# Down and output projection on two 64-row groups of TensorE, two token rows alternating, with the attention output stored 640 wide

## The chip, the cores and the metric

The kernel runs on one NeuronCore of a Trainium2 chip. The metric is device time in microseconds for one execution, inputs and outputs in HBM. TensorE does matrix products into PSUM (eight banks of 128 partitions x 512 fp32), VectorE (DVE) and ScalarE (ACT) do elementwise work and empty PSUM, GpSimd (POOL) helps at the start, and SyncE (SP) issues nearly all DMAs.

## The reference

One transformer layer with attention and feed-forward in parallel on a LayerNorm of the same input, in bf16. There are 2048 tokens (S), 576 features (D = 32 heads x 18) and a hidden size of 4608 (F).

```python
def _A_ref(x, wqkv, wo):                  # dilated local attention
    H, Dh, W, dil = 32, 18, 8, 2
    q, k, v = split(x @ wqkv)
    idx = pos[:, None] - (arange(W) * dil)[None, :]      # 8 keys: s, s-2, ..., s-14
    mask = idx >= 0
    ...
    attn = softmax(where(mask, q . k[idx] * Dh ** -0.5, -1e9))
    o = attn . v[idx]
    return o.reshape(B, S, D) @ wo

def _B_ref(x, w_gate, w_up, w_down):
    return (silu(x @ w_gate) * (x @ w_up)) @ w_down

xn = _layernorm(x)
return x + _A_ref(xn, wqkv, wo) + _B_ref(xn, w_gate, w_up, w_down)
```

## The kernel before, in words

Token 16p + r lies on partition p as row r, so a row r is a block of 128 tokens, and a shift by 2 tokens is a shift by two rows. A token tile tt is four rows (512 tokens); there are four tiles.

The kernel has a first stage and then four times two stages.

- **QKV projection** (p_row, L270), row by row. LayerNorm is done two rows ahead on DVE, and the normalized rows are transposed into xnT (feature on partition, token along the free axis). Since 576 = 4.5 x 128, the matmuls use two groups of 64 array rows: the 4.5 feature tiles are nine halves of 64, and the last 64 features stand twice in xnT, on partitions 0-63 and 64-127. ACT writes Q into QO (one row of QO is 576 features), and K and V into a ring for the attention.
- **Gate and up** (g_pair, L519), 9 chunks of four hidden blocks for each token tile. Each hidden block j needs a gate bank and an up bank. In the first sweep the lower 64 rows work on gate and the upper 64 on up; in the second sweep they change over, so that each bank receives all nine halves. Since two row groups must not write one bank at once, a fence stands between the sweeps: a POOL no-op that waits for the last matmul of the first sweep and that the first matmul of the second waits for (fence_after, fence_before). g_evac turns a finished block into hT: ACT makes sg = silu(gate) (L530) and copies up to uc (L531), DVE multiplies (L532). sg and uc have four buffers each.
- **Down and output projection** (L567, L570), after the ninth chunk of a tile. For each of the four rows and each column half h of 288, 36 matmuls of hT with wd and 5 of oT (the attention output, transposed) with wo add up in one bank, all with 128 array rows. DVE adds the residual x (L576) and SP stores the row.

oT takes the place of xnT of the same tokens. It is filled by four DMA transposes on SP (L545) when the gate stage of the tile is over; each reads 640 values from QO, that is the 576 of its row and 64 beyond it, which meet zero rows of wo (L166).

The attention itself is a chain of DVE instructions (chain): products with K (L370), sums over 18 features (L375), softmax with one exponential on ACT (L395), products with V (L402) and their sums (L407), the last of which goes back into QO. It is not written out in one piece: a queue (Filler) holds its parts with guessed costs, and dve.pump(us) emits as many parts as fit the given time, after every g_evac (1.4) and ahead of the residual addition of each row in the down stage (8.5). dve.drain emits what is left of a tile's chain ahead of its transposes. Chain tt + 1 is queued during the gate stage of tile tt, at chunk 1.

Weights for gate and up come in two slots, one chunk ahead; wd (nine parts) and wo (18 parts of 32 rows, one for each feature of a head) come in the gate stage of the first tile.

PSUM is a ring of eight banks: a g_pair takes four, a row of the down stage two.

Of the kernel before, what the change touches and what calls it, by code (L numbers as in the profile page):

```python
# [9 lines left out]
bf16 = mybir.dt.bfloat16  # L10
f32 = mybir.dt.float32
ACT = mybir.ActivationFunctionType
ALU = mybir.AluOpType
# [4 lines left out]
P = 128  # L18
H, DH, W, DIL = 32, 18, 8, 2
D = H * DH  # L20
HALF = D // 2
# [3 lines left out]
KT = 5  # L25
DPAD = KT * P
# [3 lines left out]
R = 16  # L30
RT = 4
NTT = R // RT
TT = RT * P
# [37 lines left out]
def kernel(  # L71
# [11 lines left out]
    nc = tc.nc  # L83
# [3 lines left out]
    NF = F // P  # L87
# [3 lines left out]
    out_v = out.rearrange("b (p r) d -> p (b r) d", r=R)  # L91

    const = ctx.enter_context(tc.tile_pool(name="const", bufs=1))
    big = ctx.enter_context(tc.tile_pool(name="big", bufs=1))
    tmp = ctx.enter_context(tc.tile_pool(name="tmp", bufs=1))
# [7 lines left out]
    warm = const.tile([P, 1], f32, name="warm")  # L103

    xnT = big.tile([P, KT, S], bf16, name="xnT")
    QO_t = big.tile([P, R * D + 64], bf16, name="QO")
    QO = QO_t[:, 0:R * D].rearrange("p (r d) -> p r d", d=D)
    Kr = big.tile([P, NRING, D], bf16, name="Kr")
    Vr = big.tile([P, NRING, D], bf16, name="Vr")
    hT = big.tile([P, NF, TT], bf16, name="hT")  # L110
    wd = big.tile([P, NF, D], bf16, name="wd")
    wo = big.tile([P, KT, D], bf16, name="wo")
# [5 lines left out]
    xr = big.tile([P, RT, D], bf16, name="xr")  # L118
# [16 lines left out]
    oT = xnT  # L135
# [26 lines left out]
    for c in range(1, 4):  # L162
        nc.sync.dma_start(xc_b[c], x_v[:, 4 * c:4 * c + 4, :])
    nc.scalar.activation(warm[:], eps_t[:], ACT.Sqrt)
    nc.gpsimd.memset(QO_t[:, R * D:], 0.0)
    nc.gpsimd.memset(wo[64:128, KT - 1, :], 0.0)  # L166
    for ring in (Kr, Vr):
        nc.gpsimd.dma_start(ring[0:1, 0:HALO, :], wz[0:1, :].unsqueeze(1).to_broadcast([1, HALO, D]))

# [13 lines left out]

    def load_wo(d):
        k, row = divmod(d * H, P)
        nc.sync.dma_start(wo[row:row + H, k, :], A_wo.rearrange("(h d) j -> d h j", d=DH)[d])

    def load_wd(ch):
        nc.sync.dma_start(wd[:, ch * FC:(ch + 1) * FC, :],
# [2 lines left out]
    def new_ps(name):  # L192
        return ps.tile([P, 512], f32, name=name, tag="ps")
# [91 lines left out]
    def fence_after(mm):  # L285
        f = nc.gpsimd.engine_nop()
        tc.add_manual_dep(f.ins, mm.ins.name, SYNC, reason="first half done")
        return f

    def fence_before(mm, f):  # L290
        tc.add_manual_dep(mm.ins, f.ins.name, SYNC, reason="banks change row tiles")
# [23 lines left out]
    def p_evac(r, t, between=None):  # L315
# [6 lines left out]

        nc.scalar.copy(QO[:, r, 0:G], t[0][:, 0:G])  # L323
        if between is not None:
            between()
        nc.scalar.copy(ks[:, j, HALF:D], t[2][:, 0:HALF])
        v_copy(0, 8, t[2][:, HALF:G])
        nc.scalar.copy(QO[:, r, G:D], t[1][:, 0:D - G])
        nc.scalar.copy(ks[:, j, 0:HALF], t[1][:, D - G:G])
# [23 lines left out]
    dve = Filler()  # L353
# [7 lines left out]
    def chain(tt):  # L361
        rows = slice(RT * tt, RT * tt + RT)
        prod = PP[:, 0, :].rearrange("p (r c) -> p r c", c=D)
        acc = PP[:, 1, :].rearrange("p (r d h) -> p r d h", d=DH, h=H)
        pv = PP[:, 0, :].rearrange("p (r d h) -> p r d h", d=DH, h=H)
        Lr = L.rearrange("p w r h -> p r h w")

        def mul(w):
            for a, b, s in pieces(tt, w):
                nc.vector.tensor_tensor(prod[:, a:b], QO[:, RT * tt + a:RT * tt + b, :],  # L370
                                        Kr[:, s:s + b - a, :], op=ALU.mult)

        def red(w, h):
            rs = slice(2 * h, 2 * h + 2)
            nc.vector.tensor_reduce(L[:, w, rs], prod[:, rs].rearrange("p r (h d) -> p r h d", d=DH),  # L375
                                    axis=AX.X, op=ALU.add)

        def mask():
            for w in range(1, W):
                n = min(RT, max(0, 2 * w - RT * tt))  # L380
                if n:
                    nc.vector.memset(L[0:1, w, 0:n, :], NEG)

        bc = lambda t: t[:].unsqueeze(1).to_broadcast([P, W, RT, H])
        for w in [0] + list(range(W - 1, 0, -1)):
            dve.add(1.3, lambda w=w: mul(w))
            for h in range(2):
                dve.add(1.2, lambda w=w, h=h: red(w, h))
        dve.add(0.4, mask)
        dve.add(1.2, lambda: nc.vector.tensor_reduce(mx[:], Lr, axis=AX.X, op=ALU.max))  # L390
        dve.add(1.2, lambda: nc.vector.tensor_tensor(L, L, bc(mx), op=ALU.subtract))  # L391
        if tt + 1 < NTT:
            dve.add(0.0, lambda: ring_load(1, tt + 1))
        dve.add(2.0, None)
        dve.add(1.0, lambda: nc.scalar.activation(L, L, ACT.Exp, scale=SCALE))  # L395
        dve.add(1.2, lambda: nc.vector.tensor_reduce(ssum[:], Lr, axis=AX.X, op=ALU.add))  # L396
        dve.add(0.3, lambda: nc.vector.reciprocal(ssum[:], ssum[:]))  # L397
        dve.add(1.2, lambda: nc.vector.tensor_tensor(A[:], L, bc(ssum), op=ALU.mult))  # L398

        def pvm(w, dst):  # L400
            for a, b, s in pieces(tt, w):
                nc.vector.tensor_tensor(dst[:, a:b], Vr[:, s:s + b - a, :].rearrange("p r (d h) -> p r d h", h=H),  # L402
                                        A[:, w, a:b].unsqueeze(2).to_broadcast([P, b - a, DH, H]), op=ALU.mult)

        def pva(w):
            dst = acc if w else QO[:, rows, :].rearrange("p r (d h) -> p r d h", h=H)
            nc.vector.tensor_tensor(dst, acc, pv, op=ALU.add)  # L407

        for w in range(W - 1, -1, -1):
            dve.add(1.4, lambda w=w: pvm(w, acc if w == W - 1 else pv))  # L410
            if w < W - 1:
                dve.add(1.3, lambda w=w: pva(w))
        if tt + 1 < NTT:
            dve.add(0.0, lambda: ring_load(2, tt + 1))

        def done():
            chains[0] += 1
        dve.add(0.0, done)


    def pair_stats(r):
# [37 lines left out]
    for r in range(R):  # L459
        if r == 0:  # L460
            t = p_row0(first)
        else:
            t = p_row(r, (lambda: transp_halves(r + 1)) if r <= 3 else None)
# [61 lines left out]

    def g_evac(ch, j):
        t = ring_ps[j]
        sg = tmp.tile([P, TT], bf16, name="sg", tag="sg", bufs=4)
        uc = tmp.tile([P, TT], bf16, name="uc", tag="uc", bufs=4)
        nc.scalar.activation(sg[:], t[0][:], ACT.Silu)  # L530
        nc.scalar.copy(uc[:], t[1][:])  # L531
        nc.vector.tensor_tensor(hT[:, ch * FC + j, :], sg[:], uc[:], op=ALU.mult)  # L532

    for tt in range(NTT):
        for ch in range(NCH):
            it = tt * NCH + ch
            for p in range(2):
                g_pair(tt, ch, p)
                for j in (2 * p, 2 * p + 1):
                    g_evac(ch, j)  # L540
                    dve.pump(1.4)
            if ch == NCH - 1:
                dve.drain(lambda: chains[0] > tt)
                for r in range(RT * tt, RT * tt + RT):
                    nc.sync.dma_start_transpose(oT[:, :, r * P:(r + 1) * P], QO_t[:, r * D:r * D + KT * P])  # L545
            if it + NSLOT < NTT * NCH:
                load_gu(it + NSLOT)
            if tt == 0:
                if ch == 0:
                    store(1, 3)  # L550
                    store(2, 3)
                if 1 <= ch <= 7:
                    load_wd(ch - 1)
                for _ in range(3 if ch in (1, 2) else 2):
                    if wo_order:
                        load_wo(wo_order.pop(0))
            if ch == 7:
                nc.sync.dma_start(xr[:], x_v[:, RT * tt:RT * tt + RT, :])
            if ch == 1 and tt < NTT - 1:
                chain(tt + 1)  # L560
        for sub in range(RT):
            r = RT * tt + sub
            t = [new_ps("d_ps") for h in range(2)]
            for h in range(2):
                cols = slice(h * HALF, (h + 1) * HALF)
                for f in range(NF):
                    nc.tensor.matmul(t[h][:, 0:HALF], hT[:, f, sub * P:(sub + 1) * P], wd[:, f, cols],  # L567
                                     start=(f == 0), stop=False)
                for k in range(KT):
                    nc.tensor.matmul(t[h][:, 0:HALF], oT[:, k, r * P:(r + 1) * P], wo[:, k, cols],  # L570
                                     start=False, stop=(k == KT - 1))
            dve.pump(8.5)
            ot = tmp.tile([P, D], bf16, name="ot", tag="ot", bufs=3)
            for h in range(2):
                cols = slice(h * HALF, (h + 1) * HALF)
                nc.vector.tensor_tensor(ot[:, cols], t[h][:, 0:HALF], xr[:, sub, cols], op=ALU.add)  # L576
                if r == R - 1:
                    nc.sync.dma_start(out_v[:, r, cols], ot[:, cols])
            if r < R - 1:
                nc.sync.dma_start(out_v[:, r, :], ot[:])  # L580


# [28 lines left out]
```

## Time and profile before

| | |
|---|---|
| three runs | 509.47, 511.37, 513.85 us; median 511.37 |
| profiled execution | 510.26 us, span 508.4 us, granted clock 1.0 |
| TensorE busy | 501.8 us (99%) |
| VectorE, ScalarE busy | 327.3 us (64%), 199.7 us (39%) |
| DMA | 75.01 MB, mean 148 GB/s |
| QKV stage | ends at 62.5 us |
| gate and up, each tile | 70 us |
| down and output, each tile | 40.3 us |

The span is the time from the first to the last instruction of the program in the profiled execution, which took 510.26 us in all; the median of the runs is a separate measurement. In the profile's lines, PE is TensorE's matmuls and PEld its weight loads, which run beside them; a form like 128*128 128x288 is array rows * columns, then the shape of the moving operand. Matmuls are pipelined: the duration of one (286 ns for 288 columns) is longer than the step from one to the next. The chain that ended last is followed back from the last instruction to what released it at each step.

### The profile page before, as it was taken

Reading aid. Unit: us, or ns where it says so; the run is one execution under the profiler, and the core shown is the slowest. Engines: PE = TensorE matmul, PEld = TensorE weight load, DVE = VectorE, ACT = ScalarE, POOL = GpSimd, SP = SyncE. Lnnn points to the kernel's source line nnn. Section 1 sums busy time; section 2 is a strip of 40 time slices with the busy share of each in tenths; the row PEclk is TensorE's granted clock in tenths of the full one; section 3 lists DMA queues with packets and bytes.
Section 4 is the critical chain, followed back from the end, with each engine's and each line's share of the span. In section 5 each row is a group of like instructions: output and inputs, shape, how many; then the busy total and the mean of one; then the engine's idle time right before and its main releaser. Section 6 shows DMA issues by size and latency. Waiting matters only on the chain.

```text
span 508.4 us, 10685 instructions
## 1 busy us (share of the span) xinstructions
PE 501.8 (99%) x4518; PEld 297.2 (58%) x4518; DVE 327.3 (64%) x472; ACT 199.7 (39%) x415; POOL 2.5 (0%) x10
## 2 busy tenths in 40 slices
PE   8999999999999999999999999999999999999997
PEld 3555566666677644444778544445777444445775
DVE  4984699799999789999795129996980122222010
ACT  2766556655400164555300354557000454553000
POOL 1000000000000000000000000000000000000000
PEclk9999999999999999999999999999999999999999
DMA  8889978878932036436702054455500235452000
GB/s 282 268 194 197 319 244 292 261 239 257 236 103 71 13 104 222 164 118 224 195 20 71 13 186 135 146 186 155 133 25 13 92 110 184 151 176 47 19 13 24
DMA packets 75711, 75.01 MB, mean 148 GB/s; under 512 B 21948, under 2 KB 71448, under 8 KB 75664
## 3 DMA queue, kind: packets, MB, share of 16 engines
q1 hardware_dynamic: 75232, 73.64, 47.9%
q8 instruction: 35, 0.57, 0.5%
q10 hardware_dynamic: 368, 0.66, 0.4%
q14 instruction: 12, 0.10, 0.1%
q0 software_dynamic: 64, 0.03, 0.0%
HBM read 58.69 MB, written 5.90 MB: 127 GB/s over the span
## 4 chain that ended last, share of the span: by engine, by line
PE 93%; DVE 2%; DMA 1%; ACT 1%; SPq 1%; issue 1%
PE g_ps L519 53%; PE d_ps L567 27%; PE qkv_ps L270 9%; PE d_ps L570 4%; DMA wd<-in_A_x_dram 1%; ACT uc L531 0%; DVE ssum L396 0%; SPq L144 0%; DVE stats L209 0%; SPq L147 0%; DVE hT L532 0%; ACT L395 0%; DVE PP L402 0%; DVE A L398 0%; DVE ssum L397 0%
## 5 line engine op out<-in xcount | busy, mean ns | idle before, releaser
L519 PE MATMUL g_ps<-xnT,gu 64*128 64x512 bf16 x2592 | 280.9, 376 | 0.2 <-ACT uc L531 0.2
L519 PEld LDWEIGHTS <-gu 64*128 64x128 bf16 x2592 | 138.2, 94 | 141.9 <-issue 0.7
L530 ACT ACTIVATE sg<-g_ps 128x512 bf16<-128x512 f32 x144 | 87.3, 606 | 158.5 <-PE g_ps L519 158.5
L567 PE MATMUL d_ps<-wd,hT 128*128 128x288 bf16 x1152 | 146.6, 286 | 0.5 <-DVE hT L532 0.5
L567 PEld LDWEIGHTS <-hT 128*128 128x128 bf16 x1152 | 112.4, 98 | 30.7 <-issue 1.3
L532 DVE TENSOR_TENSOR hT<-sg,uc 128x512 bf16<-128x512 bf16 x144 | 60.2, 419 | 93.4 <-ACT uc L531 93.4
L375 DVE TENSOR_REDUCE PP<-PP 128x64 f32<-128x1152 bf16 x64 | 85.1, 1346 | 0.4
L531 ACT CAST uc<-g_ps 128x512 bf16<-128x512 f32 x144 | 85.2, 592 | 0.0
L270 PE MATMUL qkv_ps<-hT,xnT 64*128 64x432 bf16 (+1 forms) x560 | 53.9, 343 | 1.2 <-DMA hT<-in_A_wqkv_dram 1.1
L576 DVE TENSOR_TENSOR ot<-d_ps,xr 128x288 bf16<-128x288 f32 x32 | 13.8, 453 | 58.6 <-PE d_ps L570 58.6
L370 DVE TENSOR_TENSOR PP<-QO,Kr 128x2304 bf16<-128x2304 bf16 (+1 forms) x35 | 43.5, 1249 | 11.5 <-DMA Kr<-hT 11.3
L402 DVE TENSOR_TENSOR PP<-Vr,A 128x2304 bf16<-128x2304 bf16 (+1 forms) x35 | 43.4, 1250 | 0.5
L270 PEld LDWEIGHTS <-xnT 64*128 64x128 bf16 (+1 forms) x560 | 28.0, 94 | 25.6 <-issue 1.8
L407 DVE TENSOR_TENSOR PP<-PP 128x2304 bf16<-128x2304 bf16 x24 | 32.5, 1354 | 0.4
L530 ACT ACT_TABLE_LOAD x5 | 6.4, 1283 | 52.4 <-PE g_ps L519 52.3
L570 PE MATMUL d_ps<-wo,xnT 128*128 128x288 bf16 x160 | 24.8, 286 | 0.0
L570 PEld LDWEIGHTS <-xnT 128*128 128x128 bf16 x160 | 15.6, 98 | 4.0
L321 ACT CAST hT<-qkv_ps 128x144 bf16<-128x144 f32 (+1 forms) x32 | 13.8, 433 | 3.8 <-DMA kv_d<-hT 2.8
L395 ACT ACTIVATE PP<-PP 128x1024 f32<-128x1024 f32 x4 | 4.2, 1057 | 27.5 <-DVE PP L391 27.5
L209 DVE BATCH_NORM_STATS2 stats<-wd 128x6 f32<-128x288 bf16 x32 | 12.7, 440 | 3.0 <-DMA wd<-in_A_x_dram 3.0
L323 ACT CAST QO<-qkv_ps 128x432 bf16<-128x432 f32 x16 | 8.3, 517 | 7.0 <-PE qkv_ps L270 7.0
L396 DVE TENSOR_REDUCE ssum<-PP 128x128 f32<-128x1024 f32 x4 | 7.7, 1918 | 2.3 <-ACT PP L395 2.3
(39 smaller groups left out, 90.0 us busy)
## 6 DMA issues: line engine op xcount, KB each, us to landing
gu<-in_B_w_gate_dram SPq DMA_DIRECT2D x36, 512.0 KB, 3.8
gu<-in_B_w_up_dram SPq DMA_DIRECT2D x36, 512.0 KB, 5.1
wd<-in_B_w_down_dram SPq DMA_DIRECT2D x9, 576.0 KB, 6.0
kv_d<-hT SPq DMA_DIRECT2D x6, 576.0 KB, 6.6
gu<-in_B_w_gate_dram SPq DMA_DIRECT2D x36, 64.0 KB, 4.8
gu<-in_B_w_up_dram SPq DMA_DIRECT2D x36, 64.0 KB, 4.5
xr<-in_A_x_dram SPq DMA_DIRECT2D x4, 576.0 KB, 5.5
out_dram<-ot SPq DMA_DIRECT2D x15, 144.0 KB, 1.8
```

The costliest lines, as they stand in the source:

```text
L270: return nc.tensor.matmul(t[g][:, 0:G], xnT[rows, kt, r * P:(r + 1) * P], w_at(g, kt, rows), start=start, stop=stop)
L321: nc.scalar.copy(vdst[:, :, lo:lo + n], src.rearrange("p (h d) -> p d h", d=DH))
L370: nc.vector.tensor_tensor(prod[:, a:b], QO[:, RT * tt + a:RT * tt + b, :], Kr[:, s:s + b - a, :], op=ALU.mult)
L375: nc.vector.tensor_reduce(L[:, w, rs], prod[:, rs].rearrange("p r (h d) -> p r h d", d=DH), axis=AX.X, op=ALU.add)
L402: nc.vector.tensor_tensor(dst[:, a:b], Vr[:, s:s + b - a, :].rearrange("p r (d h) -> p r d h", h=H), A[:, w, a:b].unsqueeze(2).to_broadcas ...
L407: nc.vector.tensor_tensor(dst, acc, pv, op=ALU.add)
L519: mm = nc.tensor.matmul(ring_ps[j][b][:], gu[rows, slot, k, fc], xnT[rows, kt, tok], start=(swap == 0 and kt == 0), stop=(swap == 1 and kt ...
L530: nc.scalar.activation(sg[:], t[0][:], ACT.Silu)
L531: nc.scalar.copy(uc[:], t[1][:])
L532: nc.vector.tensor_tensor(hT[:, ch * FC + j, :], sg[:], uc[:], op=ALU.mult)
L567: nc.tensor.matmul(t[h][:, 0:HALF], hT[:, f, sub * P:(sub + 1) * P], wd[:, f, cols], start=(f == 0), stop=False)
L570: nc.tensor.matmul(t[h][:, 0:HALF], oT[:, k, r * P:(r + 1) * P], wo[:, k, cols], start=False, stop=(k == KT - 1))
```

## The change

- The down and output projection runs on two 64-row groups. For a row, the first sweep has the lower rows at columns 0-287 and the upper rows at columns 288-575 over 36 hidden tiles and all five tiles of oT and wo; in the second sweep the groups change column halves, over 36 hidden tiles and four tiles of oT and wo. Two rows alternate: first sweep of row a, first sweep of row b, second of a, second of b. A fence through POOL stands between the two sweeps of a row.
- The last 64 features are needed on both groups. QO becomes QOP with rows of 640; at the end of a chain a DVE copy puts features 512-575 once more at 576-639, and the transposes read one row of 640. The last 64 rows of wo are loaded twice, and the two memsets on POOL go.
- sg and uc have three buffers instead of four.
- dve.pump gets 12.5 ahead of the addition of row a and 4.0 ahead of that of row b.

```diff
-    QO_t = big.tile([P, R * D + 64], bf16, name="QO")
-    QO = QO_t[:, 0:R * D].rearrange("p (r d) -> p r d", d=D)
+    QOP = big.tile([P, R, DPAD], bf16, name="QO")
+    QO = QOP[:, :, 0:D]
...
-    nc.gpsimd.memset(QO_t[:, R * D:], 0.0)
-    nc.gpsimd.memset(wo[64:128, KT - 1, :], 0.0)
...
     def load_wo(d):
         k, row = divmod(d * H, P)
-        nc.sync.dma_start(wo[row:row + H, k, :], A_wo.rearrange("(h d) j -> d h j", d=DH)[d])
+        for lo in (row, row + 64) if k == KT - 1 else (row,):
+            nc.sync.dma_start(wo[lo:lo + H, k, :], A_wo.rearrange("(h d) j -> d h j", d=DH)[d])
...
         def done():
+            nc.vector.tensor_copy(QOP[:, rows, D:DPAD], QOP[:, rows, 512:D])
             chains[0] += 1
-        dve.add(0.0, done)
+        dve.add(0.3, done)
...
-        sg = tmp.tile([P, TT], bf16, name="sg", tag="sg", bufs=4)
-        uc = tmp.tile([P, TT], bf16, name="uc", tag="uc", bufs=4)
+        sg = tmp.tile([P, TT], bf16, name="sg", tag="sg", bufs=3)
+        uc = tmp.tile([P, TT], bf16, name="uc", tag="uc", bufs=3)
...
+    def d_half(tt, sub, swap, t, fence):
+        r = RT * tt + sub
+        tiles = [(hT[:, f, sub * P:(sub + 1) * P], wd[:, f, :]) for f in range(NF)]
+        tiles += [(oT[:, k, r * P:(r + 1) * P], wo[:, k, :]) for k in range(KT - swap)]
+        if not swap:
+            t[sub] = [new_ps("d_ps") for h in range(2)]
+        for n, (a, w) in enumerate(tiles):
+            for half in range(2):
+                rows = slice(64 * half, 64 * half + 64)
+                h = half ^ swap
+                mm = nc.tensor.matmul(t[sub][h][:, 0:HALF], a[rows], w[rows, h * HALF:(h + 1) * HALF],
+                                      start=(swap == 0 and n == 0), stop=(swap == 1 and n == len(tiles) - 1))
+                if not swap and n == len(tiles) - 1 and half == 1:
+                    fence[sub] = fence_after(mm)
+                if swap and n == 0 and half == 0:
+                    fence_before(mm, fence[sub])
+
+    def d_out(r, sub, t):
+        ot = tmp.tile([P, D], bf16, name="ot", tag="ot", bufs=3)
+        for h in range(2):
+            cols = slice(h * HALF, (h + 1) * HALF)
+            nc.vector.tensor_tensor(ot[:, cols], t[h][:, 0:HALF], xr[:, sub, cols], op=ALU.add)
+            if r == R - 1:
+                nc.sync.dma_start(out_v[:, r, cols], ot[:, cols])
+        if r < R - 1:
+            nc.sync.dma_start(out_v[:, r, :], ot[:])
...
-                    nc.sync.dma_start_transpose(oT[:, :, r * P:(r + 1) * P], QO_t[:, r * D:r * D + KT * P])
+                    nc.sync.dma_start_transpose(oT[:, :, r * P:(r + 1) * P], QOP[:, r, :])
...
-        for sub in range(RT):
-            r = RT * tt + sub
-            t = [new_ps("d_ps") for h in range(2)]
-            for h in range(2):
-                cols = slice(h * HALF, (h + 1) * HALF)
-                for f in range(NF):
-                    nc.tensor.matmul(t[h][:, 0:HALF], hT[:, f, sub * P:(sub + 1) * P], wd[:, f, cols],
-                                     start=(f == 0), stop=False)
-                for k in range(KT):
-                    nc.tensor.matmul(t[h][:, 0:HALF], oT[:, k, r * P:(r + 1) * P], wo[:, k, cols],
-                                     start=False, stop=(k == KT - 1))
-            dve.pump(8.5)
...
+        for sub in range(0, RT, 2):
+            t, fence = {}, {}
+            for swap in range(2):
+                for i in (sub, sub + 1):
+                    d_half(tt, i, swap, t, fence)
+                    if swap:
+                        dve.pump(12.5 if i == sub else 4.0)
+                        d_out(RT * tt + i, i, t[i])
```

More of the change, by code (lines that the diff above doesn't have):

```diff
@@ L560 @@
                 chain(tt + 1)
-        for sub in range(RT):
-            r = RT * tt + sub
-            t = [new_ps("d_ps") for h in range(2)]
-            for h in range(2):
-                cols = slice(h * HALF, (h + 1) * HALF)
-                for f in range(NF):
-                    nc.tensor.matmul(t[h][:, 0:HALF], hT[:, f, sub * P:(sub + 1) * P], wd[:, f, cols],
-                                     start=(f == 0), stop=False)
-                for k in range(KT):
-                    nc.tensor.matmul(t[h][:, 0:HALF], oT[:, k, r * P:(r + 1) * P], wo[:, k, cols],
-                                     start=False, stop=(k == KT - 1))
-            dve.pump(8.5)
[L573 to L580, printed above, removed]
+        for sub in range(0, RT, 2):
[6 more added lines that the diff above has]
+                        d_out(RT * tt + i, i, t[i])
 _INS = ['A_x', 'A_wqkv', 'A_wo', 'B_x', 'B_w_gate', 'B_w_up', 'B_w_down']
```

## The prediction

> **What bounds the kernel now.** I read the page first: busy shares, then the chain that ended last.
>
> ```profile
> PE 501.8 (99%) x4518; PEld 297.2 (58%) x4518; DVE 327.3 (64%) x472; ACT 199.7 (39%) x415; POOL 2.5 (0%) x10
> ...
> PE 93%; DVE 2%; DMA 1%; ACT 1%; SPq 1%; issue 1%
> ```
>
> TensorE is busy for 99% of the span and makes 93% of the chain. The granted clock is 1.0 throughout. So a change is worth what it adds to or takes from TensorE's own stream, plus the tail after the last matmul. To see what one matmul costs in each stage I read the chain in order of time: start, duration, line, count.
>
> ```profile
> 18.16 0.14 PE pt L252 x10
> 18.30 3.28 PE qkv_ps L270 x36
> ...
> 138.15 4.41 PE d_ps L567 x36
> 142.56 0.61 PE d_ps L570 x5
> ...
> 173.31 70.04 PE g_ps L519 x648
> 243.35 4.52 PE d_ps L567 x36
> ...
> 504.98 0.46 DVE ot L576
> ```
>
> The stage to be changed (L567, L570) takes 4.41/36 = 122.5 ns a matmul, each using all 128 rows over 288 columns. The other three already run as pairs on two 64-row groups. A pair takes 70.04/324 = 216.2 ns at 512 columns, 3.28/18 = 182.2 ns at 432, and 0.14/5 = 28 ns at 64. These lie on a line: the pair costs its columns plus a few ns, and the two groups stream at the same time. From 64 to 432 columns the slope is 154.2/368 = 0.419 ns a column, which at 288 gives 28 + 224 x 0.419 = 121.9 ns. From 432 to 512 it is 34.0/80 = 0.425, which gives 182.2 - 144 x 0.425 = 121.0. The full-row step is 122.5. I take 122.5 for the new pair.
>
> **Part 1, fewer steps.** Before, one token row needs 2 column halves x (36 + 5) = 82 steps, and the fifth output-projection step multiplies 64 rows of zero weights. After, it needs 41 pairs in the first sweep and 40 in the second, 81. Over 16 rows that is 1312 - 1296 = 16 steps less, 16 x 122.5 = 1.96 us off the path.
>
> **Part 2, changes of shape.** The timeline of TensorE shows what the array loses when it goes from 64-row groups to full rows and back.
>
> ```profile
> 172.53 0.78 PE L570 MATMUL d_ps<-wo,xnT 128*128 128x288 bf16 x5
> 173.24 70.10 PE L519 MATMUL g_ps<-xnT,gu 64*128 64x512 bf16 x648
> 243.28 4.58 PE L567 MATMUL d_ps<-wd,hT 128*128 128x288 bf16 x36
> ```
>
> The fifth L570 starts at 172.53 + 4 x 0.1225 = 173.02, so the next step is due at 173.14; the gate matmul starts at 173.24. The last gate matmul ends at 243.34, so with its 376 ns it starts at 242.96 and the next is due at 243.18; L567 starts at 243.28. Each change costs 0.10 us. There are four into the down projection and three out of it; all seven go: 0.7 us off the path.
>
> **Part 3, the tail.** Before, the first half of the last row is added to the residual 5 us before the end, under the second half's matmuls, and only one addition (0.46) follows the last matmul. After, both halves finish in the last sweep, so two follow.
>
> ```profile
> 162.95 0.81 DVE L576 TENSOR_TENSOR ot<-d_ps,xr 128x288 bf16<-128x288 f32 x2
> ```
>
> Two in a row take 0.81: +0.35 on the path. The last store starts that much later.
>
> **Part 4, weight loads.** They double, 1312 to 2592.
>
> ```profile
> L519 PEld LDWEIGHTS <-gu 64*128 64x128 bf16 x2592 | 138.2, 94 | 141.9 <-issue 0.7
> L567 PEld LDWEIGHTS <-hT 128*128 128x128 bf16 x1152 | 112.4, 98 | 30.7 <-issue 1.3
> ```
>
> One load of L519 takes 94 ns, 2592 of them 243.6, yet they cover only 138.2 us: 106.6 ns a pair, so the two groups load side by side. 106.6 fits under a step of 122.5, as 98 does now. In the 28 ns pairs of L252 loads of the same size follow one another even faster. Cost taken: 0, hidden under the streaming; without that cover it would be up to 94 ns a pair, 122 us.
>
> A page of the Trainium skill speaks against this: "TensorE: Matmul & The Clock Gate", Part 3, says that a weight load overlaps a running matmul only if their row groups differ. By it the pair would cost 94 + 122.5 and the sum would be about 122 us worse. But L567 overlaps its 98 ns loads with matmuls of the same rows at 122.5 ns a step, so here the measurement decides against the rule.
>
> **Part 5, supply of instructions.** This is the unknown. A pair is four instructions (two loads, two matmuls). The stage now takes 2 per 122.5 ns, 16 a us; after, 4 per 122.5, 33 a us. The longest stream near that is the QKV projection, 4 per 182.2 = 22 a us, for 40 us without a gap. L252 shows 20 in 0.14 us, but that burst may come from a queue filled ahead. Bounds: 28 ns a pair (no effect) and 182.2 ns (1296 x 59.7 = +77 us). Neither QKV nor gate shows a supply limit, as both follow their columns, so I take no effect and keep the upper end.
>
> The same page, section "Back-to-back issue gap", gives about 81 ns a matmul for sustained load-and-matmul streams at 128 columns. By it a pair would take 162 ns and the kernel about 51 us more; no stream here falls below 91 ns a matmul for more than ten matmuls, so no run yet shows it.
>
> **Part 6, what lies beside.** The order of DVE's and ACT's work stays nearly the same: the four exponentials stand after 12, 36, 72 and 104 gate evictions in both, and the 0.49 us that L567 loses at 358.5 to a late hT should stay. These edits I cost at nothing:
>
> ```profile
> 133.00:173.30 40.30, 40.30 (x331) 32.02 (x332) 39.12 (x41) 3.59 (x5) 0.00 (x0) 1.00 0.29 80
> ...
> 128.09 0.97 SPq L186 DMA_DIRECT2D wo<-in_A_wo_dram  x2
> 129.10 0.42 SPq L558 DMA_DIRECT2D xr<-in_A_x_dram  x1
> 133.05 5.24 SPq L545 DMA_TRANSPOSE xnT<-QO  x4
> ```
>
> - Two more wo loads put 0.97 us on SP. Its queue is empty from 129.52 to 133.05, where the transposes wait for the last gate matmul. Uncovered, they would shift the four transposes, and so L570's first step, by 0.97. The transposes land 2.6 us after issue; the second row now needs its own at 133.0 + 5.0 + 4.4 = 142.4 instead of 147.5, and it is there at about 137.
> - The copy of 64 features, four times: the nearest DVE row (128x64, L228) is 0.18 us, four times as wide at most 0.7. Except in the first tile, DVE has 12 us or more idle in each pass. In the first it stands ahead of evictions that have 2 us in hand (last hT at 135.3, needed at 137.3).
> - sg and uc with three buffers: the fourth sg must now wait for the first multiplication. The closest place is the start of the gate stage: the multiplication ends at 70.05, the fourth sg starts at 70.42. 0.37 us of slack; elsewhere over 1 us. Lost, it costs ACT some tenths once, under 1.8 us of its own idle time per pair.
> - QO at a stride of 640: L402 reads A broadcast over 18 features in 1250 ns, L370 flat rows in 1249, so 0; at worst DVE is later where it has room.
> - Fences: a row's second sweep waits on a POOL no-op behind its first, with the other row's 5 us of matmuls between. Nothing else is behind it on POOL. All later matmuls queue behind that wait. Without the cover, two releases of 0.05 (the "issue" step of the chain ahead of the matmul at 358.55) on each of 16 rows, 1.6 us.
> - PSUM: the last row of a pass is now evicted after it, as before; its banks are due at the fourth gate group, some 5 us later. The first pass is the tight one: DVE is busy 39.12 of 40.3 us, so I expect evictions about 3 us late there, within that margin.
> - The removed POOL memsets (0.15 and 0.57 us) stand before 2 us, where TensorE only warms up and LayerNorm waits for x: 0.
>
> **The sum.** -1.96 - 0.7 + 0.35 = -2.3 us. Against the profiled execution: span 508.4 and 510.26 with what lies around it, so 508.0. The median shown is 511.37, 0.2% above that execution; on its footing the forecast is 509.1. About 1% is what a measurement of this kernel can tell from no change (its three runs spread over 4.4 us), so this is "within 1%".
>
> **Rivals.**
> - *TensorE is starved of instructions* (slower). Place: every pair of the stage. It decides from 122.5 + 2.3/1296 us = 124.3 ns a pair for break-even, and from 128 ns for over 1%. At 135 ns: +16.2 - 2.3, 525; at QKV's 182: 586. For it: 33 a us is half again what any long stage shows. Against: all streams here follow their columns to within 3 ns, and the burst runs at 28 ns. Chance 0.27.
> - *An eviction takes the place of the gain.* In the first pass DVE never rests, d_out of the fourth row comes behind 4 us of pumped work, and the gate group that reuses its banks waits. If DVE is 5 us further behind than I reckon, that is some 2 to 3 us once: 512. For it: 39.12 of 40.3. Against: the pumped total falls from 34 to 33 us a pass. Chance 0.07, of which 0.03 over 1%, if several boundaries stall.
> - *The groups run free of each other* and the pair costs the 121.0 of the second slope: another 1296 x 1.5 = 1.9 us, 507.2. With the spread between runs this can show as over 1%. Chance 0.08.
> - *The two groups don't run at once*, so that nothing is done as said: 1296 x 122.5 more, 668. The 216 ns pairs of L519 exclude it nearly; counted under the first.
>
> **How the numbers follow.** Forecast 0.58 at 509.1, own range 505 to 513. Faster by over 1%: 0.08 (the third rival). Within 1%: 0.58 + 0.04 = 0.62. Slower: 0.27 + 0.03 = 0.30. Unknown is mostly Part 5; to leave out no more than 0.2 the range must reach to a pair of about 135 ns, 526, beyond which I put half of the starved cases (0.14); below, it ends at 504.5, the third rival less a run's spread.
>
> **What would show it.** Right: eighty-one pairs a row at 122 to 123 ns, a row pair in 19.8 us against 20.1 for two rows now, a pass in 39.7 against 40.2; no gap of 0.10 at the stage's ends; weight loads covering near 107 ns of each step; two L576-like additions after the last matmul; SP, POOL and DVE ending no TensorE idle. Wrong: a step over 124 ns with no releaser, or idle TensorE put down to "issue"; an idle gap at the start of the gate stage ended by DVE; a chain through ACT or DVE longer than the half microsecond at 358.

## The result, and the profile after

The changed kernel takes 507.47 us (median of 8 runs, 506.67 to 508.64) against 511.17 (8 runs, 509.38 to 514.30). The ratio is 0.9928, with a 95% interval of 0.9906 to 0.9950: 3.7 us faster, 2.6 to 4.8. It is within the 1% called "no change" in the prediction, but clear of noise.

The profiled execution after took 508.64 us, the slowest of its eight, with a span of 506.9. So the two spans differ by only 1.5 us, and the stages have to be compared one by one. The page and its chain:

```profile
PE 499.3 (99%) x5798; PEld 349.1 (69%) x5798; DVE 327.0 (65%) x476; ACT 199.6 (39%) x415; POOL 1.9 (0%) x8
...
PE 93%; DVE 2%; DMA 2%; ACT 1%; SPq 1%; issue 0%; DVEq 0%; ACTq 0%
```

TensorE is still the bound. It has 1280 more matmuls and as many more weight loads, and is busy for less time. The chain in order of time, after (start, duration, line, count):

```profile
19.28 0.15 PE pt L251 x10
19.43 3.29 PE qkv_ps L269 x36
...
63.81 69.89 PE g_ps L519 x648
133.70 39.61 PE d_ps L546 x646
173.31 70.01 PE g_ps L519 x648
243.32 39.61 PE d_ps L546 x646
...
357.83 0.05 issue
357.87 35.58 PE d_ps L546 x578
393.45 69.93 PE g_ps L519 x648
463.38 39.71 PE d_ps L546 x648
503.09 0.02 issue
503.11 0.46 DVE ot L557
```

(A pass is the down stage of one token tile. The trace has all 648 matmuls of a pass; the chain counts 646 in two of them, because the first gate matmul starts ahead of the last output projection, and the time of that last pair goes to the gate stage's piece. So 39.61/323 = 122.6 ns a pair, and the pass of 648 gives 39.71/324 = 122.6; the passes that the later runs show whole take 39.69, 122.5 a pair. The 122.3 and 39.6 in the expectations below divide the short piece by 324.) The sum is not touched by this: the second pass with the gate stage ahead of it takes 70.01 + 39.61 = 109.62 us, where the kernel before took 70.04 + 40.28 = 110.32. The QKV stage ends 1.3 us later in this execution than in the one before, because its first loads came later; that is what hides half of the gain in the spans. From the start of the first gate matmul to the end of the last matmul it is 439.6 us, 442.8 before; the first gate stage before is 0.5 us longer than the others by a wait (62.51 to 133.02 in its chain), so not all of that difference comes from the change.

The ends of the stage, in the timeline of TensorE after:

```profile
172.74 0.57 PE L546 MATMUL d_ps<-wo,xnT 64*128 64x288 bf16 x6
173.10 0.38 PE L519 MATMUL g_ps<-xnT,gu 64*128 64x512 bf16 x1
173.15 0.28 PE L546 MATMUL d_ps<-wo,xnT 64*128 64x288 bf16 x1
173.27 70.09 PE L519 MATMUL g_ps<-xnT,gu 64*128 64x512 bf16 x647
243.03 4.61 PE L546 MATMUL d_ps<-wd,hT 64*128 64x288 bf16 x71
```

A gate matmul starts on one group (173.10) before the other group's last output projection (173.15): there is no break any more. The groups of weight loads (busy us in all and mean ns of one, then the idle time ahead and what ended it):

```profile
L519 PEld LDWEIGHTS <-gu 64*128 64x128 bf16 x2592 | 173.7, 94 | 105.6
...
L546 PEld LDWEIGHTS <-hT 64*128 64x128 bf16 x2304 | 128.5, 94 | 15.5 <-DVE hT L532 0.9
```

2304 loads of 94 ns would be 216.6 us one after the other; they cover 128.5. How far they overlap differs between executions, 112.2 us in the changed kernel's second profile and 143.1 in the last run, while an undisturbed pass takes 39.69 in both: the loads don't set the pace. The tail (in brackets the idle time ahead):

```profile
503.11 0.82 DVE L557 TENSOR_TENSOR ot<-d_ps,xr 128x288 bf16<-128x288 f32 x2 [4.08 <-PE d_ps L546]
```

Two additions follow the last matmul, 0.82 us where it was 0.46.

### The profile page after: what moved, and what is told of

Read it like the earlier page. It is cut to its first block, busy times and chain, and to the rows that moved or that the text cites. A ratio compares the mean times of both kernels' runs of the same rounds, so it can differ in the third digit from the quotient of the medians.

```text
span 506.9 us, 13258 instructions
## 1 busy us (share of the span) xinstructions
PE 499.3 (99%) x5798; PEld 349.1 (69%) x5798; DVE 327.0 (65%) x476; ACT 199.6 (39%) x415; POOL 1.9 (0%) x8
## 4 chain that ended last, share of the span: by engine, by line
PE 93%; DVE 2%; DMA 2%; ACT 1%; SPq 1%; issue 0%; DVEq 0%; ACTq 0%
PE g_ps L519 54%; PE d_ps L546 30%; PE qkv_ps L269 9%; DMA wd<-in_A_x_dram 2%; SPq L147 0%; DVE ssum L395 0%; SPq L144 0%; ACT uc L531 0%; DVE stats L208 0%; DVE hT L532 0%; ACT L530 0%; ACT L394 0%; DVE PP L401 0%; DVE A L397 0%; DVE ssum L396 0%
## 5 line engine op out<-in xcount | busy, mean ns | idle before, releaser
L519 PEld LDWEIGHTS <-gu 64*128 64x128 bf16 x2592 | 173.7, 94 | 105.6
L546 PE MATMUL d_ps<-wd,hT 64*128 64x288 bf16 x2304 | 149.2, 283 | 0.6 <-DVE hT L532 0.6
L546 PEld LDWEIGHTS <-hT 64*128 64x128 bf16 x2304 | 128.5, 94 | 15.5 <-DVE hT L532 0.9
L269 PE MATMUL qkv_ps<-hT,xnT 64*128 64x432 bf16 (+1 forms) x560 | 54.1, 343 | 2.0 <-DMA hT<-in_A_wqkv_dram 1.8
L269 PEld LDWEIGHTS <-xnT 64*128 64x128 bf16 (+1 forms) x560 | 29.2, 94 | 25.3 <-issue 2.7
L546 PE MATMUL d_ps<-wo,xnT 64*128 64x288 bf16 x288 | 25.4, 283 | 0.0
L546 PEld LDWEIGHTS <-xnT 64*128 64x128 bf16 x288 | 17.0, 94 | 1.8
```

Of the source, the lines that this page charges most:

```text
L269: return nc.tensor.matmul(t[g][:, 0:G], xnT[rows, kt, r * P:(r + 1) * P], w_at(g, kt, rows), start=start, stop=stop)
L519: mm = nc.tensor.matmul(ring_ps[j][b][:], gu[rows, slot, k, fc], xnT[rows, kt, tok], start=(swap == 0 and kt == 0), stop=(swap == 1 and kt ...
L546: mm = nc.tensor.matmul(t[sub][h][:, 0:HALF], a[rows], w[rows, h * HALF:(h + 1) * HALF], start=(swap == 0 and n == 0), stop=(swap == 1 and ...
```

## The experiments

All ratios are to the kernel before, run on the same chip in the same job; its median was 511.3 to 513.0 us there. The changed kernel's ratio is 0.9928 (0.9906 to 0.9950), and 0.9916 (0.9888 to 0.9943) when it ran again. For that second run 0.993 to 0.995 had been expected if TensorE's stream is all of the gain, 0.992 or less if the start of the kernel or the side edits give something too; the interval covers both. Parts of some tenths of a us are read from the traces, where a gate stage and a pass without waits repeat to 0.02 us from run to run. The sum of a gate stage and the pass after it is the measure: 110.32 before, 109.62 after.

**1. The half tile not saved.**

```diff
-        tiles += [(oT[:, k, r * P:(r + 1) * P], wo[:, k, :]) for k in range(KT - swap)]
+        tiles += [(oT[:, k, r * P:(r + 1) * P], wo[:, k, :]) for k in range(KT)]
```

> The changed kernel with the half tile not saved: both sweeps of a row take five tiles of oT and wo, so 82 pairs a row instead of 81 (the last 64 features are counted twice in the output). If the saved step is worth its streaming, as reckoned: 16 x 122.3 ns = 2.0 us slower than the changed kernel, each down pass 40.1 us instead of 39.6. If the gain comes with the shape changes or the side edits alone: no difference to the changed kernel.

509.60 us, ratio 0.9967 (0.9941 to 0.9994). Its chain:

```profile
173.18 69.93 PE g_ps L519 x648
243.11 40.18 PE d_ps L546 x656
```

110.11, that is 0.49 more than the changed kernel, and 4 x 0.49 = 1.96 us in all: four more pairs a pass at 122.5. The same two lines also give the other part: against the kernel before, with the same number of steps, 110.32 - 110.11 = 0.21 us remain for two changes of shape.

**2. The half tile saved alone**, in the kernel before with the side edits of experiment 4, the last rows of wo loaded twice and both memsets out.

```diff
-                for k in range(KT):
-                    nc.tensor.matmul(t[h][:, 0:HALF], oT[:, k, ...], wo[:, k, cols], start=False, stop=(k == KT - 1))
+                for k in range(KT - 1):
+                    nc.tensor.matmul(t[h][:, 0:HALF], oT[:, k, ...], wo[:, k, cols], start=False, stop=False)
+            for h in range(2):
+                rows = slice(64 * h, 64 * h + 64)
+                nc.tensor.matmul(t[h][:, 0:HALF], oT[rows, KT - 1, ...], wo[rows, KT - 1, cols of h], start=False, stop=True)
```

> The kernel before, with full-row matmuls, that saves the half tile alone: 40 full steps for each column half, then one pair of 64-row matmuls for the last 64 features of both halves. 81 steps a row, but eight changes of shape a pass where there were two. If each change costs 0.10 us, a pass is 324 x 0.1225 + 8 x 0.10 = 40.5 us and the kernel is 0.0 to 0.6 us slower than before. If the changes of shape cost nothing and the saved step is the whole gain: a pass of 39.7 and 2 to 2.6 us faster than before.

511.44 us, ratio 1.0014 (0.9991 to 1.0036). In its chain (L574 is the new pair):

```profile
252.20 0.49 PE d_ps L570 x4
252.69 0.23 PE d_ps L574 x2
252.92 4.52 PE d_ps L567 x36
257.44 0.49 PE d_ps L570 x4
257.93 4.41 PE d_ps L567 x36
```

The pair takes 0.23 where a step is 0.12, and the first 36 after it 4.52 where 4.41 is the streaming: about 0.11 lost at each change. The four saved steps of a pass (0.49) go into the six more changes: an undisturbed pass takes 40.54 (132.16 to 172.70 in its chain), with a gate stage of 69.93 that is 110.47, 0.15 more than before. So the step count alone gives nothing; it pays only because the whole stage keeps one shape.

**3. Changes of shape put back into the changed kernel.**

```diff
-        tiles = [(hT[:, f, ...], wd[:, f, :]) for f in range(NF)]
+        tiles = [(hT[:, f, ...], wd[:, f, :]) for f in range(1, NF)]
         if not swap:
             t[sub] = [new_ps("d_ps") for h in range(2)]
+            for h in range(2):
+                nc.tensor.matmul(t[sub][h][:, 0:HALF], hT[:, 0, ...], wd[:, 0, cols of h], start=True, stop=False)
```

> The changed kernel with the first hidden tile of each row done by two full-row matmuls in place of its two pairs: the same 81 steps a row, but two changes of shape for every row, 32 more in all. At 0.10 us each, as read at the stage's ends: 3.2 us slower than the changed kernel, passes of 40.4 instead of 39.6. If those 0.10 us came from something else at the stage's ends (waits for hT or for banks): no difference.

511.14 us, ratio 1.0014 (0.9988 to 1.0040): the gain is gone. In the chain, L543 are the full rows:

```profile
173.94 69.93 PE g_ps L519 x648
243.87 0.35 PE d_ps L543 x2
244.22 5.00 PE d_ps L549 x80
249.23 0.35 PE d_ps L543 x2
```

Two full steps take 0.35 instead of 0.245. The pass runs from 243.87 to 284.41, 40.54 us, so stage and pass are 110.47, 0.85 above the changed kernel, for eight changes: 0.106 us each, 3.4 us in all.

**4. The side edits alone**, twice. The kernel before with QOP, the copy, three buffers and without the memset of QO:

```diff
+    QOP = big.tile([P, R, DPAD], bf16, name="QO")
+    QO = QOP[:, :, 0:D]
...
-    nc.gpsimd.memset(QO_t[:, R * D:], 0.0)
...
+            nc.vector.tensor_copy(QOP[:, rows, D:DPAD], QOP[:, rows, 512:D])
...
-        sg = ... bufs=4
+        sg = ... bufs=3        # and uc
```

> The kernel before with the side edits alone: QO stored 640 wide with the DVE copy, three buffers for sg and uc, one POOL memset less; the matmuls of the down stage as before. As reckoned, all of it is hidden: the same as before within 0.5 us, passes of 40.3. The rival: the part of the 3.7 us that the traces of TensorE do not show (about 0.9) comes from these edits; then 0.5 to 1.0 us faster than before.

> The kernel before with the side edits alone, a second time, since the first interval, 0.9951 to 1.0008, left open whether they give up to 0.9 us. If they are hidden, as its trace says (passes of 40.29 as before): a ratio of 1.000 within its interval. If they give 0.9 us: 0.998.

510.03 us, 0.9980 (0.9951 to 1.0008), and 511.53 us, 0.9992 (0.9963 to 1.0021). Neither tells them from nothing. In both traces the gate stage is 70.04 us and an undisturbed pass 40.29, as before. So they don't touch TensorE's stream; a gain of up to half a per cent in the stage before it is not excluded.

**5. The two rows not alternating.**

```diff
-            for swap in range(2):
-                for i in (sub, sub + 1):
+            for i in (sub, sub + 1):
+                for swap in range(2):
                     d_half(tt, i, swap, t, fence)
                     if swap:
-                        dve.pump(12.5 if i == sub else 4.0)
+                        dve.pump(8.5)
```

> The changed kernel with the two sweeps of a row one straight after the other, so that the fence through POOL has no other row's matmuls to hide it (the pumped work is 8.5 us ahead of each row's addition, as before). If the fence is exposed, each of 16 rows loses the end of its last pair (283 - 122 = 160 ns) and two releases of some 50 ns: 0.26 x 16 = 4 us slower than the changed kernel. If the fence costs nothing by itself: no difference.

512.58 us, ratio 1.0009 (0.9985 to 1.0034): all of the gain is lost. In its chain the sweep of 82 matmuls is followed by the fence:

```profile
243.18 5.04 PE d_ps L546 x82
248.22 0.05 issue
248.26 0.02 POOLq L285
248.28 0.05 issue
248.33 6.79 PE d_ps L546 x107
```

and in its waits (total us, times, longest)

```profile
PEld L546 <- POOLq L285: 7.0, 16, 0.4
```

Its pass is 243.18 to 284.09, 40.91 against 39.69: 1.22 us for four rows, 0.3 a row, 4.9 in all. It was reckoned at 4. The alternation is what makes the new form pay.

**6. Narrower matmuls, for the supply of instructions.**

```diff
-            for half in range(2):
+            for part in range(2):            # 4 in the second run
+                for half in range(2):
...
+                    c0, c1 = part * HALF // 2, (part + 1) * HALF // 2
-                mm = nc.tensor.matmul(t[sub][h][:, 0:HALF], a[rows], w[rows, h * HALF:(h + 1) * HALF], ...)
+                    mm = nc.tensor.matmul(t[sub][h][:, c0:c1], a[rows], w[rows, h * HALF + c0:h * HALF + c1], ...)
```

> The changed kernel with every matmul of the down stage cut into two of 144 columns, each with its own weight load: 2592 pairs, twice the instructions, the same streaming. If a pair follows its columns (28 + 80 x 0.419 = 61.5 to 62.5 ns): 1 to 4 us slower than the changed kernel, passes of 39.8 to 40.5. If the supply of instructions has its limit at what the QKV stage sustained (22 a us, 182 ns a pair): 310 us slower. A limit in between shows as a constant step c with a pass of 648 x c. By the figure of 81 ns a matmul in the Trainium skill (TensorE: Matmul & The Clock Gate, section Back-to-back issue gap) a pair would be 162 ns and the kernel 260 us slower.

> The same with four matmuls of 72 columns each: 5184 pairs, four times the instructions. If a pair still follows its columns (28 + 8 x 0.419 = 31.4 to 32.5 ns): 4 to 10 us slower than the changed kernel, passes of 40.7 to 42.1. If loads and matmuls are supplied no faster than some rate, the step rests at it: at 62 ns a pair, a pass is 80 us and the kernel 160 us slower. This run and the one with 144 columns tell how far the changed kernel's 122 ns a pair is from that limit.

With 144 columns: 514.09 us, ratio 1.0026 (0.9996 to 1.0056), about 1% over the changed kernel and a little above the 1 to 4 us expected. The last pass of its chain, and its waits (total, times, longest):

```profile
469.38 40.52 PE d_ps L548 x1296
```

```profile
PEld L548 <- issue: 2.6, 3, 1.3
```

40.52/648 = 62.5 ns a pair, as the columns say, at 64 instructions a us. The first two passes have a gap of 1.15 or 1.3 us each and take 41.9 and 41.8, which is what goes beyond the expectation. With 72 columns: 649.21 us, ratio 1.270 (1.263 to 1.276). Its timeline of TensorE, with the idle time ahead of each group in brackets, and its waits:

```profile
285.17 2.25 PE L548 MATMUL d_ps<-wd,hT 64*128 64x72 bf16 x128 [2.02 <-issue]
290.27 2.25 PE L548 MATMUL d_ps<-wd,hT 64*128 64x72 bf16 x128 [2.85 <-issue]
```

```profile
PEld L548 <- issue: 116.5, 73, 3.1
```

The limit is there, and it isn't a longer step (time without a releaser is put down to "issue"). The pairs still follow their columns, 128 matmuls in 2.25 us with the last one's pipeline, and then TensorE stands for 1.2 to 2.9 us. In most rounds this comes every 128 matmuls, that is 256 instructions with their loads. The queue of instructions on the three pages (before, after, 72 columns) says what 256 are:

```profile
q8 instruction: 35, 0.57, 0.5%
```

```profile
q8 instruction: 45, 0.74, 0.6%
```

```profile
q8 instruction: 106, 1.74, 1.1%
```

From before to after there are 2 x 1280 = 2560 more instructions and 10 more packets: 256 a packet of 16 KB. From there to 72 columns it is 2 x 7776 more instructions and 61 more packets, 255 a packet. At 72 columns a packet's worth takes 3.5 to 4 us in most rounds (592.67, 596.41, 599.88, 603.63 are starts in its chain), some 70 instructions a us. So the supply is bounded by how fast packets of instructions come. That it is the fetch itself is read from these counts; no run changed the fetch. At 33 a us the changed kernel has a factor of two in hand.

**7. The last tile's chain a chunk later**, twice.

```diff
-            if ch == 1 and tt < NTT - 1:
+            if ch == (2 if tt == 2 else 1) and tt < NTT - 1:
                 chain(tt + 1)
```

> The changed kernel with the attention chain of the last tile queued one chunk later (chunk 2 instead of 1, in the third tile only), so that its exponential falls behind the last gate eviction of that tile instead of four evictions ahead of it. If the 0.6 us for which the third down pass waits for hT comes from that exponential and its two table loads: that wait goes and the kernel is 0.5 to 0.7 us faster than the changed kernel. If not, or if later work in the chain makes another wait: no difference, or slower.

> The version with the last tile's attention chain queued one chunk later, beside the changed kernel on one chip. If the wait at the start of the third down pass was the exponential's: 0.6 to 0.9 us faster than the changed kernel, third pass 39.7 us as the others. If the wait is hidden by something else: the same.

506.92 us, ratio 0.9899 (0.9867 to 0.9930), and 507.73 us, 0.9928 (0.9899 to 0.9957). Beside the changed kernel's 507.38 in the second job that is no difference that can be measured. The trace shows that the wait is gone: the third pass, without the break at 358,

```profile
282.75 69.93 PE g_ps L519 x648
352.68 39.69 PE d_ps L546 x648
```

and gate stage and pass are 109.62 where the changed kernel takes 110.52 there. The 0.9 us gained is less than the starts differ: in the second job's profile of this version the first gate matmul starts at 67.24, in the others between 61 and 64. The weights of the QKV projection are not the reason: in this profile they have landed at 11.28, in the last run's at 11.29, and there the first gate matmul starts at 62.52. What differs is the granted clock. From 10 to 15 us this profile has (busy time and count of PE, PEld, DVE, ACT and POOL, then the clock, the share of the DMA engines and GB/s):

```profile
10.00:15.00 5.00, 3.68 (x11) 1.55 (x11) 0.00 (x0) 0.00 (x0) 0.00 (x0) 0.50 0.95 300
```

The first 12 matmuls of L269 take 4.48 us there, 2.35 in the first profile of this version, where the clock is 1.00. From 20 us on it is 1.00 in both.

**8. A wait that the first pass has in some executions.** The changed kernel's second profile shows it, in the chain:

```profile
62.26 69.95 PE g_ps L519 x648
132.23 4.66 DMA xnT<-QO
136.93 35.45 PE d_ps L546 x576
```

TensorE stands 0.5 us at 136.9 for the first transposed row. The first profile after has SP's queue in the same order:

```profile
128.81 2.02 SPq L185 DMA_DIRECT2D wo<-in_A_wo_dram  x4
132.36 0.35 SPq L587 DMA_DIRECT2D xr<-in_A_x_dram  x1
133.77 5.24 SPq L574 DMA_TRANSPOSE xnT<-QO  x4
```

Behind the four wo loads xr is issued at 132.36, 1.4 us ahead of the transposes; before it was 129.10, 4 us ahead. Of the delay 1.5 us is a wait that SP's own waits put down to a load of gu, and that the kernel before doesn't have. The first transpose lands behind xr: 136.89, after xr at 136.30, in the execution with the wait; 136.28, after xr at 135.65, in the kernel before, where L570 needed it at 137.4. In all twelve traces with xr ahead of the transposes, other than that with 72 columns, it lands 0.58 to 0.69 us after xr. The last run took both waits out:

```diff
+            if ch == 7:
+                nc.sync.dma_start(xr[:], x_v[:, RT * tt:RT * tt + RT, :])
             if tt == 0:
...
-            if ch == 7:
-                nc.sync.dma_start(xr[:], x_v[:, RT * tt:RT * tt + RT, :])
-            if ch == 1 and tt < NTT - 1:
+            if ch == (2 if tt == 2 else 1) and tt < NTT - 1:
```

> The changed kernel with two edits: the last tile's attention chain queued one chunk later, and the load of xr issued ahead of the four wo loads of its chunk instead of behind them. In the profiles of the changed kernel's kind xr is issued some 1.4 us ahead of the transposes and the first transpose lands 0.6 us after it, 4.1 to 4.7 us after its own issue; in those of the kernel before it lands 3.2 to 3.6 us after. If the two more wo loads do this by pushing xr back, the first transpose lands 3.6 us or less after its issue, the first down pass has no wait (0 to 0.5 us in the profiles so far) and is 39.7 us. The third pass is 39.7 too. TensorE from the first gate matmul to the last one: 438.5 to 439.0 us; against before a ratio of 0.989 to 0.992. If the transposes are late for another reason, they land as late as before.

506.86 us, ratio 0.9909 (0.9881 to 0.9937). No pass has a wait, and from the first gate matmul to the last matmul it is 438.8 us, as expected; the changed kernel's two profiles have 439.6 and 439.9. But the transposes land 3.84 us after issue, not 3.6: now the wo loads are just ahead of them (the last one lands at 136.50, the first transpose at 136.68). They land behind what was issued last. So pushing xr back is at most one way to be late. That the two more wo loads cause it is not shown either: with two of them the first transpose lands 3.2 to 3.6 us after its issue in three traces, with four 3.5 to 4.7 at 288 columns, and two of those with four, experiment 2 (3.67) and experiment 5 (3.49), are about as early as with two. No run has the changed kernel with two. This version is the best by its trace, by 0.7 to 1.1 us; by time it can't be told from the changed kernel.

## Why the prediction was right, point by point

The forecast was -2.3 us and 509.1; measured are -3.7 (-4.8 to -2.6) and 507.47. The range and the side were right; the size is at two thirds of the measured one, just outside the interval. The terms of the sum came out one by one, as follows; that the median moved by more than their sum is not explained by them.

- **The pair's step** (122.5 ns, reckoned between 121.0 and 122.5): 122.5. The line through the pairs of 64, 432 and 512 columns held, and at 144 (62.5) it holds too.
- **Fewer steps, 1.96**: 1.96 by experiment 1.
- **Changes of shape, 0.10 each, 0.7 in all**: 0.106 by experiment 3, 0.21 for two by experiment 1.
- **The tail, 0.35**: 0.82 - 0.46 = 0.36.
- **Weight loads, hidden**: right; with 144 columns they are hidden under 62.5 ns as well. The Trainium skill's rule that loads overlap running matmuls only of other row groups ("TensorE: Matmul & The Clock Gate", Part 3) does not hold for this kernel: before, full-row loads of 98 ns went under full-row matmuls at 122.5 ns a step.
- **Supply of instructions**, the main rival at 0.27: refuted at 33 a us, though the limit is real, near 70. The same page's 81 ns a matmul (section "Back-to-back issue gap") is above what the 144-column run held for a whole pass: 62.5 ns from one matmul of a row group to the next, 31 ns a matmul over both groups.
- **Fences, hidden by the other row**: right; the price without the cover was put at 1.6 us and is 4.9. The price left out the end of the last pair, which must come out of the pipeline before the release (in the expectation of experiment 5 it is in).
- **Two more wo loads, cost nothing**: open, and the argument for it had a hole. I checked that SP's queue was empty until the transposes, and that the wo loads fit there. I did not ask where xr, which stands behind them, would go, and that the transposes follow it; and the 2.6 us from issue to landing is the middle value, while the first transpose of the first pass took 3.2. Of the two profiles of the changed kernel one has no wait for it, the other 0.5 us; experiment 8 leaves open whether the wo loads are the cause.
- **Three buffers**: the 0.37 us of slack was used up: ACT waits 0.3 us once for DVE, at the fourth sg as said, and TensorE doesn't notice.

```profile
ACT sg L530 <- DVE hT L532: 0.3, 1, 0.3
```

- **Evictions about 3 us late in the first pass**: about 2.0, 1.7, 1.9 and 0.4 us (the additions start at 150.60, 155.24, 170.35 and 173.74; the rows end after 122, 162, 284 and 324 pairs of the pass), and no gate matmul waits. The wait for hT at 358 stayed, as said; in gate stage and pass together it costs 0.90 and 0.78 us in the changed kernel's two profiles, 0.67 before.

```profile
PE d_ps L546 <- DVE hT L532: 0.6, 1, 0.6
```

- **The third rival**, a pair of 121.0 ns and 507.2 us, is nearer to the measured 507.47 than the forecast, but by chance: the pair takes 122.5.

What stays open is the remainder. The sums of gate stage and pass differ by 0.70 us each, 2.8 for the four tiles; less 0.1, as no change of shape follows the last pass, and less the tail of 0.36, that is 2.3, the forecast. Whole executions show a little more, with waits that come and go: three profiles with the down stage of before take 442.8, 442.2 and 443.1 us from the first gate matmul to the last one (the first and the third have 0.5 and 0.9 us more in the first gate stage), two of the changed kernel 439.6 and 439.9; with the tail that is a gain of about 2.5, just under the lower ends of the two measured intervals (2.6 and 2.9). Another 1 to 2 us of the medians would have to lie outside this stretch.

The clocks on record show a part of it. In the job in which the changed kernel ran again, 14 of the 27 executions of the kernel before have a mean granted clock under 0.998, of the changed kernel 1 of 10, and those of the kernel before are 2.8 us longer in the median than its others; the profile with 0.50 in experiment 7 is of such an execution, and there the time goes in the first 20 us. Among executions at 0.998 or more the medians of that job are 510.8 before, 509.8 with the side edits alone and 507.2 after; in the job of experiment 4's first run they are 510.6 before and 510.0 with the side edits. So at one clock the change gives 3.6 us, and 0.7 to 0.9 of that would be the side edits', which were costed at nothing; 0.2 of it lies outside the span (execution less span, on average: 1.97 us before, 1.79 with the side edits, 1.80 after). This is not shown: the executions were sorted afterwards, only 10 and 6 with the side edits are left, their whole ratios (0.9980, 0.9992) reach 1, and no run has the changed kernel without them.

## What to carry to other kernels

Using two row groups doesn't make TensorE faster: a pair costs what one full step costs. It saves the zero half of a contraction that isn't a multiple of 128, and the 0.1 us at each change of shape, so it is worth most where the neighbouring stages are already in that shape, and nothing where it is put in for one step. It needs independent work between the two sweeps: exposed, the fence cost 0.3 us a row and took all of the gain. Whoever adds a small load to a queue should look at the load behind it, and at who waits for that one; here the first transpose landed close behind xr in twelve of the fourteen traces, though the added loads weren't shown to make it late. And a gain of 2 to 4 us is of the order by which executions at a lower granted clock differ from the others (2.8 us in the median), so the stages have to be compared, not only the medians.

## What the runs showed of the hardware that I had not expected

- TensorE's instructions come in packets of 16 KB, 256 instructions. At 64 a us they arrive in time but for single gaps of about 1.2 us; asked for at over 120 a us (four per 33 ns), TensorE stops for 1.2 to 2.9 us after nearly each packet and settles at about 70 a us. A kernel of 72-column matmuls is 27% slower for it, with a clock of 0.985 and no releaser but "issue".
- Full rows and 64-row groups can't follow each other freely: 0.106 us for each change, in either direction.
- The two row groups keep the offset with which they start. In the first two passes of the first profile one matmul follows the other by 41 and 82 ns in turn, from the first pair to the last; behind the wait at 358 by 2 to 4 and some 120, as in all of the second profile. A pair takes 122.5 either way. With an offset one group can be in the next stage (173.10) while the other is still in this one (173.15).
